# Batch 1's queries loaded in 128-byte blocks and turned by VectorE, and TensorE's opening pauses filled to the end, in a packed-attention and expert-layer kernel

## The chip, the cores and the metric

The kernel runs on one core of a Trainium2 chip, as one launch. The metric is the device time of that launch in microseconds. The core has five engines that run side by side, each through its own list of instructions in order: TensorE (PE, with its weight loads PEld), VectorE (DVE), ScalarE (ACT), GpSimd (POOL) and SyncE (SP), whose list here issues most of the DMA transfers. They wait for each other with semaphores.

## The reference, cut to what matters

Eight batches of eight heads, 576 tokens of 64 values, 32 packed queries `p`. The packed queries attend to the keys and values; then every token's query attends to the packed result, which is both key and value. The output is the input of an expert layer with one expert per token.

```python
def sm_attn(qq, kk, vv):
    s = scale * np.matmul(qq, kk.transpose(0, 1, 3, 2))
    s = s - np.max(s, axis=-1, keepdims=True)
    a = np.exp(s)
    a = a / (np.sum(a, axis=-1, keepdims=True) + 1e-09)
    return np.matmul(a, vv)
p_packed = sm_attn(p, k, v)
x = sm_attn(q, p_packed, p_packed)            # then heads side by side: [8, 576, 512]

logits = np.einsum('bsd,de->bse', x, w_gate)  # 8 experts
# per token s: fresh = argmax of its logits; it keeps the expert of the token before it
# where its local gate is 0.5 or more, else it takes the fresh one; e is that expert
p = softmax(logits[b, s])
h = np.maximum(x[b, s] @ w1[e], 0.0)          # 512 -> 1024
out[b, s] = p[e] * (h @ w2[e])                # 1024 -> 512
```

All is float32. With the inputs used, every token of a batch ends with the expert of that batch's first token, so a batch takes one expert's weights; a branch behind the main part handles others.

## The kernel before

Each batch goes through three parts.

- **Preparation.** Heads are taken in two groups of four, called Q = 0 and 1 in the code ("quads"). Keys and queries are needed with the 64 head values on partitions, so they are turned. `scores` multiplies packed queries and keys (L415), `keys` raises them (ScalarE, L448), turns the weights on TensorE (L458, copies L460), multiplies them with the values (L470), divides (L478, tile `zz`) and turns the result (L485, copy L488, tile `ppT`). `queries` multiplies that with the turned queries (L511, and L520 for the gate), turns the scores on VectorE (L529, tile `sT`), runs a softmax over the 32 packed entries (L540 maximum, L542 subtraction, L544 exponential, L548 to L554 sum and division) and turns them back (L560 or L562, tile `a2t`). `a2t` is split in two numbers of TensorE's fast float format: `a2h` (ScalarE, L568) and the rest `a2l` (L571).
- **The gate.** `gates` (L658, L666) multiplies `a2t` with the gate's weights and picks the expert; `choose` (L601, L604) puts its number in a register of SP. `weights` then loads that expert's first layer `w1t` (L757) and eight pieces of the second, `w2raw` (L766). `pack_weights` multiplies the first layer with `ppT` (L783), casts it (ScalarE, L790, `wph`) and takes the rest (VectorE, L793, `wpl`). For batch 0 an `early_choice` from the first token alone starts the loads sooner.
- **The expert layer,** the main part: `chunks` goes over eight chunks of 128 hidden units. A chunk's first layer is two times six matmuls of 288 tokens (L806), then ScalarE and VectorE split the result in `h` (L816, L821); the second layer is fifteen matmuls or so (L845, L850, L854) with `w2raw` split by L832 (ScalarE) and L834 (VectorE).

The order of every engine's list is set when the kernel is built. `weave` holds threads (generators); each says with `need(...)` what it waits for, a `Clock` with prices for each instruction estimates when that is ready, and `weave` steps the thread that is ready, preferring the main part while it has credit. So a change in one thread moves the rows of others. PSUM has eight banks: three named `bank` for everything short, `acc0` to `acc4` for the second layer's sums, of which `acc1` to `acc3` serve as banks too until the main part begins. A tile of SBUF has a fixed number of buffers per name (`BUFS`: "kv" 4, "qn" 3, "w2raw" 8, "p_in" 2), and a load waits for its buffer.

There are two ways to load and turn keys and queries. `load_tokens` reads a quad with runs of 1,536 bytes into "kv", 576 KB each; `turn_tokens` then turns a head with three TensorE transposes (L365) into a bank, and ScalarE copies it (L369) into "qn". `load_blocks` reads all eight heads with runs of 128 bytes straight into "qn", four transfers of 288 KB; VectorE then turns the 32 by 32 blocks in place (L383 for keys, L496 for queries), one instruction per quad. Batch 0 (`early`) turns its keys on VectorE in tokens form (L351) and its queries by `turn_tokens`; batch 1 (`second`) uses `turn_tokens` for both; batches 2 to 7 use blocks for both. Tokens and blocks leave the tokens in different orders, and L560 and L562 put them right.

`keep_warm` (L214) puts matmuls of zeros into TensorE's list: ten at the start (`WARM`), and, while the main part has not begun, some whenever the planner finds nothing ready: the pause until the next thread is ready, divided by `FILL`.

```python
if x is None:
    x = min(when, key=when.get)
    if at_batch[0] < 0:
        keep_warm(max(0, int((when[x] - now) / FILL)))
    now = max(now, when[x])
```

`now` moves on with every such step, also where the step is not TensorE's. The `Clock` prices such a matmul at about 228 ns.

Of the kernel before, what the change touches and what calls it, by code (L numbers as in the profile page):

```python
# [35 lines left out]

FIRST_BACKLOG = 1400.0

WARM, FILL = 10, 400.0

LAT, SAME = 160.0, 127.0
START, FIRST_LOAD = 5400.0, 1700.0
# [6 lines left out]
FIRST_W2 = {"v": 2, "q": 4}  # L49
# [109 lines left out]
def packed_attn_moe_kernel(  # L159
# [17 lines left out]
    clock = Clock()  # L177
# [138 lines left out]
    def loads(st):  # L316

        b = st["b"]
        if st["early"]:
            st["p"] = load_packs(b, (nc.sync, nc.scalar, nc.scalar))  # L320

            clock.rate = 100.0
            with nc.allow_non_contiguous_dma(reason="512 elements"):
                nc.scalar.dma_start(out=q0[:, :, 0:1], in_=q[0, :, 0:1, :].rearrange("h s d -> d h s"))
            nc.scalar.dma_start(out=wgl[:, :, 0:E], in_=w_gate.rearrange("(h d) e -> d h e", d=D))
            nc.scalar.dma_start(out=wgl[:, :, E:E + 1], in_=w_local.rearrange("(h d) e -> d h e", d=D))
            order = (("k", 0), ("k", 1), ("v", 0), ("v", 1), ("q", 0), ("q", 1))
        else:
            if isinstance(b, int):
                yield need(when=lambda: "loaded" in sts[b - 1] and (b < 2 or "ereg" in sts[b - 2]))  # L330
            order = (("p", 1), ("k", 0), ("k", 1), ("v", 0), ("v", 1), ("q", 0), ("q", 1)) if st["second"] else \
                (("v", 0), ("v", 1), ("p", 1), ("k", 1), ("q", 1))
        for name, Q in order:
            blocks = name in "kq" and not (st["early"] or st["second"])
            if st["second"] and name in FIRST_W2:
                yield need(when=lambda: len(sts[0].get("w2", ())) >= FIRST_W2[name])
            yield need(slot="p_in" if name == "p" else "qn" if blocks else "kv")
            if name == "p":
                st["p"] = load_packs_by_half(b)
                continue  # L340
            x = {"k": k, "v": v, "q": q}[name]
            if blocks:
                st[name] = load_blocks(x, b)
            else:
                st[name, Q] = load_tokens(x, b, Q)
        st["loaded"] = True
# [152 lines left out]
    def queries(st, Q):  # L499
# [54 lines left out]
        nc.vector.tensor_tensor(out=sf, in0=sf, in1=sm.unsqueeze(2).broadcast_to([128, G, NP]), op=ALU.mult)  # L554
        yield need(sT)
        for r in range(2):
            if st["early"] or st["second"]:

                out = a2t.rearrange("a (p i c r) -> a r c p i", p=TP // 32, i=32, c=J3)[:, r]
                nc.vector.transpose(out=out, in_=sT[:, r].rearrange("a (c p) n -> a c p n", c=J3))  # L560
            else:
                nc.vector.transpose(  # L562
                    out=a2t.rearrange("a (m r) -> a r m", r=2)[:, r],
                    in_=sT[:, r].rearrange("a m n -> a (m n)"),
                )
# [182 lines left out]
    def weights(st):  # L748
        yield need(when=lambda: "ereg" in st)
        er = st["ereg"]  # L750
        src = w1[bass.ds(er, 1)].rearrange("o (h x) f -> x (o h) f", h=HQ)
        st["w1"], st["w2"] = [], []
        for fh in range(2):
            yield need(slot="w1t")
            clock.rate = 330.0
            w1t = tile_([128, HQ, 512], F32, "w1t")
            nc.sync.dma_start(out=w1t, in_=src[:, :, 512 * fh:512 * fh + 512])  # L757
            st["w1"].append(w1t)
        for c in range(NC):
            if st.get("early"):  # L760

                yield need(when=lambda: all(c < n or (x, 1) in sts[1] for x, n in FIRST_W2.items()))
            yield need(slot="w2raw")
            raw = tile_([128, DM], F32, "w2raw")
            clock.rate = 330.0
            nc.sync.dma_start(out=raw, in_=w2[bass.ds(er, 1), 128 * c:128 * c + 128, :].rearrange("o r f -> r (o f)"))  # L766
            st["w2"].append(raw)
# [181 lines left out]
    def weave(main):  # L949
# [3 lines left out]
        while main in threads or any(x.batch < 0 for x in threads):  # L953
# [4 lines left out]
            while started < B and started <= max(at_batch[0], 0) + AHEAD:  # L958
                st = sts[started]
                threads.extend(Thread(g, started) for g in (  # L960
                    slots(st), pack_weights(st), *((early_choice(st),) if started == 0 else ()),
                    *((turn_keys(st, 0), turn_keys(st, 1)) if started != 1 else (turn_keys(st, 0), turn_tokens(st, "k"))), scores(st, 0), scores(st, 1), keys(st, 0), keys(st, 1), gate_weights(st) if started == 0 else None, gates(st), *((turn_queries(st, 0), turn_queries(st, 1)) if started > 1 else (turn_tokens(st, "q"),)), queries(st, 0), queries(st, 1),
                ) if g is not None)
                threads.insert(0, Thread(weights(st), started, True))
                started += 1
# [14 lines left out]
            if x is None:  # L980
                x = min(when, key=when.get)
                if at_batch[0] < 0:
                    keep_warm(max(0, int((when[x] - now) / FILL)))
                now = max(now, when[x])
            before = clock.products
            x.step()
# [110 lines left out]
```

## Time and profile before

| | |
|---|---|
| median of 3 runs | 440.71 us (440.34 to 441.14) |
| the profiled execution | 440.03 us |
| its span, first to last instruction | 438.2 us |
| mean granted TensorE clock | 0.984 |
| TensorE busy | 417.8 us, 95% |
| VectorE, ScalarE, GpSimd busy | 303.9, 183.5, 24.9 us |
| moved by DMA | 73.16 MB, mean 167 GB/s |

The profile is of one execution. A line names the source line (L365), the engine, the operation, and output<-input by the names in the code. Times in a timeline are from the span's start; the bracket gives the engine's idle time ahead of the row and what ended it. The "granted clock" is the share of its full clock that TensorE was given. A float32 matmul shows as two records (two passes), a transpose by matmul as one.

### The profile page before, as it was taken

Reading aid. Unit: us, or ns where it says so; the run is one execution under the profiler, and the core shown is the slowest. Engines: PE = TensorE matmul, PEld = TensorE weight load, DVE = VectorE, ACT = ScalarE, POOL = GpSimd, SP = SyncE. Lnnn points to the kernel's source line nnn. Section 1 sums busy time; section 2 is a strip of 40 time slices with the busy share of each in tenths; the row PEclk is TensorE's granted clock in tenths of the full one; section 3 lists DMA queues with packets and bytes.
Section 4 is the critical chain, followed back from the end, with each engine's and each line's share of the span. In section 5 each row is a group of like instructions: output and inputs, shape, how many; then the busy total and the mean of one; then the engine's idle time right before and its main releaser. Section 6 shows DMA issues by size and latency. Waiting matters only on the chain.

```text
span 438.2 us, 10127 instructions
## 1 busy us (share of the span) xinstructions
PE 417.8 (95%) x3928; PEld 326.9 (75%) x3929; DVE 303.9 (69%) x831; ACT 183.5 (42%) x424; POOL 24.9 (6%) x41
## 2 busy tenths in 40 slices
PE   7968999999999999999999999999999999999993
PEld 6756778758866787588876787587876788688882
DVE  4587469876986798648984898648985798444331
ACT  1544534454435553535425553435424453443231
POOL 0000002100110011000110011000110002000000
PEclk9896999999999999999999999999999999999998
DMA  8989699899939995999269991999455210921003
GB/s 191 233 266 259 174 148 137 327 182 226 96 121 321 133 142 179 349 131 194 94 220 240 177 194 49 347 140 141 157 187 186 81 43 10 351 96 37 0 1 114
DMA packets 153942, 73.16 MB, mean 167 GB/s; under 512 B 123680, under 2 KB 132896, under 8 KB 153888
## 3 DMA queue, kind: packets, MB, share of 16 engines
q1 hardware_dynamic: 151760, 72.30, 75.5%
q8 instruction: 33, 0.54, 0.6%
q10 hardware_dynamic: 2128, 0.15, 0.4%
q14 instruction: 21, 0.17, 0.2%
HBM read 63.00 MB, written 9.44 MB: 165 GB/s over the span
## 4 chain that ended last, share of the span: by engine, by line
PE 88%; DVE 5%; DMA 3%; issue 1%; ACT 1%; SPq 0%; POOLq 0%; DVEq 0%; POOL 0%; ACTq 0%
PE acc L845 40%; PE bank L806 24%; PE acc L850 4%; PE bank L783 3%; DMA kv<-in_k_dram 3%; PE acc L854 3%; PE bank L470 3%; PE bank L415 2%; PE bank L458 2%; PE bank L511 2%; PE bank L658 1%; DVE wpl L793 1%; PE bank L365 1%; DVE a2t L560 1%; PE acc L214 0%
## 5 line engine op out<-in xcount | busy, mean ns | idle before, releaser
L845 PE MATMUL acc<-w2s,h 128*128 128x512 f32 x768 | 207.7, 402 | 0.0
L845 PEld LDWEIGHTS acc<-w2s,h 128*128 128x128 f32 x768 | 135.1, 188 | 30.6 <-issue 8.3
L816 ACT ACTIVATE h<-bank 128x288 fp32r<-128x288 f32 x128 | 52.7, 412 | 117.9 <-PE bank L806 108.1
L821 DVE SCALAR_TENSOR_TENSOR h<-bank,h 128x288 fp32r<-128x288 f32 (+2 forms) x192 | 61.3, 347 | 50.1 <-ACT h L816 49.3
L806 PEld LDWEIGHTS bank<-a2h,wph 128*128 128x128 f32 x256 | 47.0, 191 | 23.9 <-issue 3.6
L806 PE MATMUL bank<-a2h,wph 128*128 128x288 f32 x256 | 57.9, 308 | 5.5 <-DVE wpl L793 1.8
L806 PE MATMUL bank<-a2l,wph 128*128 128x288 f32 x256 | 55.5, 299 | 0.0
L806 PE MATMUL bank<-a2h,wpl 128*128 128x288 f32 x256 | 55.3, 298 | 0.0
L834 DVE TENSOR_TENSOR w2s<-w2raw,w2s 128x512 fp32r<-128x512 f32 x64 | 47.7, 745 | 8.3 <-ACT w2s L832 8.2
L806 PEld LDWEIGHTS bank<-a2l,wph 128*128 128x128 f32 x256 | 41.7, 191 | 0.0
L806 PEld LDWEIGHTS bank<-a2h,wpl 128*128 128x128 f32 x256 | 41.7, 191 | 0.0
L832 ACT CAST w2s<-w2raw 128x512 fp32r<-128x512 f32 x64 | 39.4, 616 | 0.2
L571 POOL TENSOR_TENSOR a2l<-a2t,a2h 128x576 fp32r<-128x576 f32 x14 | 20.5, 1462 | 328.7 <-ACT a2h L568 328.7
L793 DVE TENSOR_TENSOR wpl<-bank,wph 128x512 fp32r<-128x512 f32 x31 | 20.1, 685 | 13.3 <-ACT wph L790 13.3
L790 ACT CAST wph<-bank 128x512 fp32r<-128x512 f32 x31 | 16.7, 590 | 28.0 <-PE bank L783 26.9
L850 PE MATMUL acc<-w2s,h 128*128 128x512 f32 x64 | 26.9, 420 | 0.0
L854 PE MATMUL acc<-w2s,h 128*64 128x512 f32 x64 | 25.3, 395 | 0.0
L783 PE MATMUL bank<-w1t,ppT 64*32 64x512 f32 x248 | 17.4, 601 | 2.7 <-DVE sm L550 1.6
L529 DVE STREAM_TRANSPOSE sT<-bank 128x288 f32<-128x288 f32 x30 | 12.8, 462 | 10.1 <-ACT gate L527 9.4
L448 ACT ACTIVATE a<-a,nb 128x576 f32<-128x576 f32 x16 | 12.5, 779 | 14.9 <-DVE nb L433 14.9
L460 ACT COPY a1T<-bank 96x384 f32<-96x384 f32 x28 | 13.3, 477 | 10.5 <-PE bank L458 10.0
L383 DVE STREAM_TRANSPOSE qn<-qn 128x1152 f32<-128x1152 f32 x12 | 16.4, 1364 | 0.1
(146 smaller groups left out, 434.7 us busy)
## 6 DMA issues: line engine op xcount, KB each, us to landing
w1t<-in_moe_w_dram SPq DMA_DIRECT2D x16, 1024.0 KB, 6.3
w2raw<-in_moe_w_dram SPq DMA_DIRECT2D x64, 256.0 KB, 7.7
kv<-in_v_dram SPq DMA_DIRECT2D x16, 576.0 KB, 10.7
out_dram<-o SPq DMA_DIRECT2D x32, 256.0 KB, 3.8
qn<-in_k_dram SPq DMA_DIRECT2D x24, 288.0 KB, 7.5
qn<-in_q_dram SPq DMA_DIRECT2D x24, 288.0 KB, 6.9
kv<-in_k_dram SPq DMA_DIRECT2D x4, 576.0 KB, 6.9
kv<-in_q_dram SPq DMA_DIRECT2D x4, 576.0 KB, 11.2
```

The costliest lines, as they stand in the source:

```text
L571: eng.tensor_tensor(out=a2l, in0=a2t, in1=a2h.bitcast(F32), op=ALU.subtract)
L783: nc.tensor.matmul(out=ts[Q][32 * h:32 * h + 32, :], lhsT=st["ppT"][Q][rows, 32 * h:32 * h + 32], rhs=w1t[rows, h], start=True, stop=True,)
L790: nc.scalar.copy(out=hi[:, Q], in_=ts[Q])
L793: nc.vector.tensor_tensor(out=lo[:, Q], in0=ts[Q], in1=hi[:, Q].bitcast(F32), op=ALU.subtract)
L806: nc.tensor.matmul(out=t[:, :HALF], lhsT=st["wp"][c // 4][wi][:, Q, fs], rhs=a2[ai][Q][:, ts], start=(n == 0), stop=(n == 5),)
L816: nc.scalar.activation(out=h[:, HALF * half:HALF * half + HALF], in_=t[:, :HALF], func=AF.Relu)
L821: nc.vector.scalar_tensor_tensor(out=h[:, dst:dst + z - a], in0=t[:, a:z], scalar=0.0, in1=h[:, HALF * half + a:HALF * half + z].bitcast(F32),
L832: nc.scalar.copy(out=w[:, 0], in_=raw)
L834: nc.vector.tensor_tensor(out=w[:, 1], in0=raw, in1=w[:, 0].bitcast(F32), op=ALU.subtract)
L845: nc.tensor.matmul(out=acc, lhsT=hs[hi], rhs=w[:, wi], start=(c == 0 and n == 0), stop=(c == NC - 1 and n == 2),)
L850: nc.tensor.matmul(out=acc, lhsT=h[:, 512:S + TAIL], rhs=w[:, 0], start=(c == 0), stop=False, skip_group_check=True,)
L854: nc.tensor.matmul(out=acc[0:TAIL], lhsT=h[:, 512:S], rhs=w[:, 1], start=False, stop=(c == NC - 1), skip_group_check=True,)
```

## The change

Five edits, shown whole. Batch 1's queries are one load in blocks (`load_blocks`, tile "qn") instead of two in tokens; they are turned by `turn_queries` (two L496 on VectorE) instead of `turn_tokens`; its `a2t` is written by L562 instead of L560, in block order; the wait of batch 0's weight loads is for that new load. And a pause is counted from TensorE's own planned end instead of `now`, in pieces of 240 ns instead of 400.

```diff
-WARM, FILL = 10, 400.0
+WARM, FILL = 10, 240.0
...
-            order = (("p", 1), ("k", 0), ("k", 1), ("v", 0), ("v", 1), ("q", 0), ("q", 1)) if st["second"] else \
+            order = (("p", 1), ("k", 0), ("k", 1), ("v", 0), ("v", 1), ("q", 1)) if st["second"] else \
                 (("v", 0), ("v", 1), ("p", 1), ("k", 1), ("q", 1))
         for name, Q in order:
-            blocks = name in "kq" and not (st["early"] or st["second"])
+            blocks = name in "kq" and not st["early"] and not (st["second"] and name == "k")
...
         for r in range(2):
-            if st["early"] or st["second"]:
+            if st["early"]:
...
             if st.get("early"):
 
-                yield need(when=lambda: all(c < n or (x, 1) in sts[1] for x, n in FIRST_W2.items()))
+                yield need(when=lambda: all(c < n or x in sts[1] for x, n in ((("v", 1), FIRST_W2["v"]), ("q", FIRST_W2["q"]))))
...
-                    ... *((turn_queries(st, 0), turn_queries(st, 1)) if started > 1 else (turn_tokens(st, "q"),)), ...
+                    ... *((turn_queries(st, 0), turn_queries(st, 1)) if started else (turn_tokens(st, "q"),)), ...
...
                 if at_batch[0] < 0:
-                    keep_warm(max(0, int((when[x] - now) / FILL)))
+                    keep_warm(max(0, int((when[x] - clock.engine("PE")) / FILL)))
```

What it moves is seen in the lists of instructions. The names are tiles with a running number; in the first two pairs the bank's own number stands ahead of the underscore, and the bracket names the engines or DMA queues that a row waits for.

TensorE, from the last filling to the main part's first rows. Before:

```order
L214 MATMUL acc4_66<-warm_64 128x128 x5
L783 MATMUL bank1_565<-w1t_453,ppT_313 32x512 [waits DMAHW3_49,Activation_49]
L783 MATMUL bank1_565<-w1t_453,ppT_313 32x512 x3
L783 MATMUL bank2_566<-w1t_453,ppT_324 32x512 [waits Activation_49]
L783 MATMUL bank2_566<-w1t_453,ppT_324 32x512 x3
L806 MATMUL bank0_583<-a2h_123,wph_533 128x288 [waits DVE_49,Activation_49]
```

And now:

```order
L214 MATMUL acc4_66<-warm_64 128x128 x10
L783 MATMUL bank2_620<-w1t_472,ppT_331 32x512 [waits DMAHW3_49,Activation_49]
L783 MATMUL bank2_620<-w1t_472,ppT_331 32x512 x3
L783 MATMUL bank0_621<-w1t_472,ppT_342 32x512 [waits DVE_49]
L783 MATMUL bank0_621<-w1t_472,ppT_342 32x512 x3
L806 MATMUL bank1_632<-a2h_123,wph_565 128x288 [waits DVE_49,Activation_49]
```

Ten fillings stand there instead of five, and the last L783 writes bank0, which VectorE's first L793 (of `bank0_567`) has to read first.

VectorE at the same place. Before:

```order
L793 TENSOR_TENSOR wpl_534<-bank0_535,wph_533 128x512 [waits PE_49]
L793 TENSOR_TENSOR wpl_534<-acc1_536,wph_533 128x512 [waits PE_49]
L793 TENSOR_TENSOR wpl_564<-bank1_565,wph_563 128x512 [waits Activation_49]
L793 TENSOR_TENSOR wpl_564<-bank2_566,wph_563 128x512 [waits Activation_49]
L834 TENSOR_TENSOR w2s_590<-w2raw_455,w2s_590 128x512 [waits DMAHW4_49,Activation_49]
```

And now:

```order
L793 TENSOR_TENSOR wpl_566<-bank0_567,wph_565 128x512 [waits PE_49]
L793 TENSOR_TENSOR wpl_566<-bank1_568,wph_565 128x512 [waits PE_49]
L834 TENSOR_TENSOR w2s_639<-w2raw_474,w2s_639 128x512 [waits DMAHW4_49,Activation_49]
L793 TENSOR_TENSOR wpl_615<-bank2_620,wph_614 128x512 [waits PE_49]
L793 TENSOR_TENSOR wpl_615<-bank0_621,wph_614 128x512 [waits PE_49]
```

L834 has moved ahead of the last two L793. Its ScalarE partner L832 still stands behind all four L790.

TensorE in batch 0's expert layer, where batch 1 is prepared. Before:

```order
L845 MATMUL acc_643<-w2s,h 128x512 x3
L470 MATMUL bank_795<-kv,a1T 32x64 x24
L365 MATMUL bank_824<-ident,kv 128x96 x3
L845 MATMUL acc_662<-w2s,h 128x512 x3
L485 MATMUL bank_848<-ident,zz 128x128
L365 MATMUL bank_853<-ident,kv 128x96 x3
L845 MATMUL acc_680<-w2s,h 128x512 x3
L365 MATMUL bank_862<-ident,kv 128x96 x3
L511 MATMUL bank_866<-qn,ppT 32x288 x4
```

And now:

```order
L845 MATMUL acc_693<-w2s,h 128x512 x3
L458 MATMUL bank_826<-ident,a_618 96x128 x3
L845 MATMUL acc_712<-w2s,h 128x512 x3
L845 MATMUL acc_730<-w2s,h 128x512 x3
L470 MATMUL bank_842<-kv,a1T 32x64 x24
L806 MATMUL bank_870<-a2h,wph 128x288 x2
L806 MATMUL bank_870<-a2l,wph 128x288 x2
L806 MATMUL bank_870<-a2h,wpl 128x288 x2
L485 MATMUL bank_877<-ident,zz 128x128
```

The eight groups of L365 that turned batch 1's queries are gone, and the rows around them stand closer.

More of the change, by code (lines that the diff above doesn't have):

```diff
@@ L961, in weave @@
                     slots(st), pack_weights(st), *((early_choice(st),) if started == 0 else ()),
-                    *((turn_keys(st, 0), turn_keys(st, 1)) if started != 1 else (turn_keys(st, 0), turn_tokens(st, "k"))), scores(st, 0), scores(st, 1), keys(st, 0), keys(st, 1), gate_weights(st) if started == 0 else None, gates(st), *((turn_queries(st, 0), turn_queries(st, 1)) if started > 1 else (turn_tokens(st, "q"),)), queries(st, 0), queries(st, 1),
+                    *((turn_keys(st, 0), turn_keys(st, 1)) if started != 1 else (turn_keys(st, 0), turn_tokens(st, "k"))), scores(st, 0), scores(st, 1), keys(st, 0), keys(st, 1), gate_weights(st) if started == 0 else None, gates(st), *((turn_queries(st, 0), turn_queries(st, 1)) if started else (turn_tokens(st, "q"),)), queries(st, 0), queries(st, 1),
                 ) if g is not None)
```

## The prediction

> **What bounds the kernel now.** I read the page first: busy times and the slices of the granted clock.
>
> ```profile
> span 438.2 us, 10127 instructions
> ...
> PE 417.8 (95%) x3928; PEld 326.9 (75%) x3929; DVE 303.9 (69%) x831; ACT 183.5 (42%) x424; POOL 24.9 (6%) x41
> ...
> PEclk9896999999999999999999999999999999999998
> ```
>
> TensorE works 95% of the span, so a matmul taken out of the main part is worth its own time, and a busy VectorE or DMA costs only where TensorE waits. TensorE is idle for 20.4 us (438.2 - 417.8), and apart from the last slice the clock row has its dips in slices 2 and 4 (11 to 22 and 33 to 44 us). So the second view is the busy time in stretches. I set their edges where the clock changes, 3.4 us apart.
>
> ```profile
> 8.06:11.47 3.41, 2.42 (x98) 1.00 1.09 212
> 11.47:14.88 3.41, 3.41 (x30) 0.50 1.10 235
> ...
> 28.50:31.94 3.44, 1.90 (x23) 1.00 1.05 396
> 31.94:35.35 3.41, 1.60 (x21) 1.00 1.07 305
> 35.35:38.77 3.42, 2.62 (x11) 0.50 1.07 257
> 38.77:42.18 3.41, 3.41 (x42) 0.50 1.08 264
> ```
>
> The columns are the stretch, its length, TensorE's busy time and instructions, granted clock, DMA share and GB/s. The clock is whole or half. It fell behind a stretch with 1.60 us of matmul and did not fall behind one with 1.90. It also fell behind 2.42 us at 8.06, where 96 of the 98 records are small 32x32 score matmuls. The half-clock stretches end behind one that was full (3.41 of 3.41). So three stretches run at half clock, and the two from 35.35 are the start of the main part.
>
> The third view is TensorE in order of time through the opening (start, length, idle before it).
>
> ```profile
> 1.09 6.18 PE L214 MATMUL acc<-warm 128*128 128x128 f32 x38 [1.09 <-DVE warm L207]
> ...
> 8.80 1.15 PE L415 MATMUL acc<-kv,p_in 32*32 32x192 f32 x48 [1.53 <-DVE p_in L351]
> ...
> 10.62 1.32 PE L415 MATMUL bank<-kv,p_in 32*32 32x192 f32 x48 [0.25 <-DVE kv L351]
> 11.87 1.65 PE L214 MATMUL acc<-warm 128*128 128x128 f32 x6
> 13.31 1.49 PE L458 MATMUL acc<-ident,a 128*96 128x128 f32 x6
> ...
> 15.70 1.55 PE L470 MATMUL bank<-kv,a1T 96*32 96x64 f32 x96
> ...
> 23.57 0.44 PE L365 MATMUL acc<-ident,kv 96*128 96x96 f32 x3 [1.28 <-DMA kv<-in_k_dram]
> ...
> 31.06 1.38 PE L214 MATMUL acc<-warm 128*128 128x128 f32 x10
> ```
>
> A warm-up matmul is two records. Ten records take 1.38 us at full clock: five at about 0.23, and the last one's tail. At half clock it is near twice that (six records in 1.65).
>
> **The change, part by part.** *More filling before the scores.* The list of instructions has 30 warm-ups instead of 19 ahead of the first scores, then 3 for 1, 7 for 3 and one more. The 11 extra end the first run at about 9.8 instead of 7.27, and the pipelined scores start near 9.5, not 8.80. With 3 warm-ups between, the second scores go from 10.62 to about 11.2, and the 7 at full clock (1.6 us) bring L458 to 14.0 against 13.31. Against that, 8.06:11.47 is now full, so I expect no half clock at 11.47. L458 up to the start of L470 took 2.39 us, nearly all at half clock; at full clock with two warm-ups it is about 1.7, so L470 starts at 15.7 as before. The cover for an error of some tenths is the transfer of batch 1's keys: TensorE waited 1.28 us for it at 23.57, the DMA share is above 1 in those stretches, and the transfers ahead of it keep the queues full. I take 0, bounds -0.3 and +0.7.
>
> *From 24.75 to the first hidden-layer product.* VectorE sets the end here.
>
> ```profile
> 24.75 0.48 DVE L529 STREAM_TRANSPOSE sT<-acc 128x288 f32<-128x288 f32 x1 [0.96 <-PE bank L511]
> ...
> 25.52 1.37 DVE L540 TENSOR_REDUCE mx<-sT 128x18 f32<-128x576 f32 x2
> ...
> 35.32 0.68 DVE L793 TENSOR_TENSOR wpl<-bank,wph 128x512 fp32r<-128x512 f32 x1
> ...
> 37.71 0.68 DVE L834 TENSOR_TENSOR w2s<-w2raw,w2s 128x512 fp32r<-128x512 f32 x1
> ```
>
> And ScalarE, in the same form:
>
> ```profile
> 34.66 1.07 ACT L790 CAST wph<-bank 128x512 fp32r<-128x512 f32 x2
> 35.62 0.63 ACT L832 CAST w2s<-w2raw 128x512 fp32r<-128x512 f32 x1
> ```
>
> In the new order the first L540 stands ahead of L529 and fills the idle 0.96; the chain up to the first L793 gets about 0.6 shorter (half of 1.37, less a wait for ScalarE), so that L793 ends at 35.4 instead of 36.0. But the new order makes two waits. The last L783 now goes into bank0, which the first L793 has to free; before, it had a bank of its own and ran at 33.54. And L834 stands ahead of the last two L793, and waits for L832, which stands behind the last L790 on ScalarE.
>
> ```profile
> 33.54 1.09 PE L783 MATMUL bank<-w1t,ppT 64*32 64x512 f32 x16 [1.10 <-DMA w1t<-in_moe_w_dram]
> ...
> 39.30 1.08 PE L658 MATMUL bank<-a2t,gate 128*32 128x128 f32 x16
> ...
> 40.52 0.85 PE L806 MATMUL bank<-a2h,wph 128*128 128x288 f32 x2
> ...
> 42.13 0.89 PE L845 MATMUL acc<-w2s,h 128*128 128x512 f32 x3
> ```
>
> So: last L783 35.45 to 36.5 (1.09 was for two halves side by side, and one alone is hardly shorter), L790 to 37.1, L832 to 37.7, L834 to 38.4, L793 to 39.0. The first six L806 run meanwhile; the second six need the bank that this L793 frees, at 39.05. Six L806 cost 1.61 at half clock (40.52 to 42.13), so 0.8 at full; the gate matmuls 1.22 (39.30 to 40.52), so 0.6. With the clock whole, L845 starts at 39.05 + 0.8 + 0.6 + 0.8 = 41.25, 0.9 earlier than 42.13.
>
> Is it whole? The 10 warm-ups for 5 between the pairs of L783, and half of the last pair gone, leave 31.94:35.35 with about 1.6 + 0.85 = 2.45 us: no fall at 35.35. The next stretch then holds one L783 half (1.05) and six L806 (0.8): 1.85, between the 1.60 that fell and the 1.90 that didn't, and its L783 use half of the rows. I hold a fall at 38.77 for likelier than not. Then the second L806 (1.6) and the gate (1.2) run at half clock to 41.85, the third ends at 42.8, 0.7 later than before. The Trainium skill ("TensorE: Matmul & The Clock Gate", Part 1) states that the clock halves after at least one idle window of about 3.4 us. By that rule no stretch here would fall and the first sum, -0.9, holds; but the trace disagrees, with falls behind stretches that held 1.60 and 2.42 us of matmul.
>
> *Batch 1's queries.* Eight groups of three transposes leave TensorE, and eight copies leave ScalarE, which has room.
>
> ```profile
> 48.08 0.41 PE L365 MATMUL bank<-ident,kv 96*128 96x96 f32 x3
> 48.27 0.47 PE L850 MATMUL acc<-w2s,h 128*128 128x512 f32 x1
> ...
> 51.13 0.53 PE L806 MATMUL bank<-a2h,wph 128*128 128x288 f32 x2 [0.51 <-ACT a1T L460]
> ...
> 53.43 0.88 PE L470 MATMUL bank<-kv,a1T 96*32 96x64 f32 x48
> ...
> 56.36 0.41 PE L365 MATMUL bank<-ident,kv 96*128 96x96 f32 x3
> 56.71 0.72 PE L511 MATMUL bank<-qn,ppT 64*32 64x288 f32 x16
> ...
> 58.17 0.53 PE L806 MATMUL bank<-a2h,wph 128*128 128x288 f32 x2 [0.73 <-ACT qn L369]
> ```
>
> A group costs from 0.19 (48.08 to 48.27) to 0.35 us (56.36 to 56.71); the eight add up to 1.9, between 1.5 and 2.8. The 0.73 waited for such a copy and goes; the 0.51 waited for a copy that now has the ScalarE queue to itself, and six L806 stand elsewhere. Together -1.24, bound 0 if other bank waits take their place. VectorE gets two turns:
>
> ```profile
> L496 DVE STREAM_TRANSPOSE qn<-qn 128x1152 f32<-128x1152 f32 x12 | 16.4, 1369 | 0.0
> ```
>
> That is 2 x 1.37 = 2.7 us, less what the plainer a2t transposes save, on an engine that is idle for 31% of the span: 0, bound +2.7.
>
> The load of 1.18 MB (8 x 576 x 64 values) changes from two pieces in "kv" to four in "qn" with runs of 128 bytes (columns: stretch, length, clock, DMA share, GB/s):
>
> ```profile
> 34.00:44.00 10.00, 0.66 1.08 248
> ...
> 48.00:56.00 8.00, 1.00 0.40 95
> 58.00:72.00 14.00, 1.00 1.42 140
> ```
>
> 1.18 MB at 140 GB/s (58 to 72, nearly all block loads) are 8.4 us; from 34 to 44, with token and weight loads, the rate is 248, or 4.8. So the queries, and the four second-layer loads behind them on SP, land some 3.6 us later than before: with the old load the engines were quiet from 48, so at up to 51.6. The cover is the quiet stretch from 48 to 56 and that chunk 4's weights are used behind 56. What SP has next, batch 2's values, waited for a "kv" slot and now has one. I take 0.
>
> *The seam to batch 1.* Both pairs of L783 now stand nearly side by side just ahead of batch 1's first L806, and half of the second waits for the first's L793: about 1.1 us of stall and of work no longer side by side. Before, it had idle times of 0.47 and 0.25:
>
> ```profile
> 91.96 0.53 PE L806 MATMUL bank<-a2h,wph 128*128 128x288 f32 x2 [0.47 <-DVE zz L478]
> ...
> 95.48 0.54 PE L806 MATMUL bank<-a2h,wph 128*128 128x288 f32 x2 [0.25 <-DVE wpl L793]
> ```
>
> So +0.4, bounds 0 and +1.
>
> **The sum.** -1.9 - 1.24 + 0.4 = -2.74, and the opening: +0.7 with one half-clock stretch, together -2.06; -0.9 without, -3.6. The profiled execution took 440.03 (span 438.2 and 1.83 around it), 0.68 below the median of the runs, 440.71. On that median: 438.65, and 437.1.
>
> **The rivals.** *No half clock at all* (1.85 us is enough, or the windows lie otherwise): 437.1. For it, the 1.90 that held. By the Trainium skill's rule above it would be this case.
> *Half clock from 35.35 as before*: L783 alone takes 2.1, the chain reaches 40.0, half-clock products follow, L845 starts at 43.5, 1.4 later: -1.35, 439.4. Against it, the filling.
> *What leaves TensorE comes back as waits*: the two turns of 1.37 us stand in VectorE's row ahead of the products' second halves (L821) that free the banks. If TensorE paid them whole, -2.06 + 2.74 = +0.7, 441.4: no change. Against it, TensorE has almost 2 us of other rows there.
> *The queries land late* (the other side): VectorE takes its rows in turn, and the first L496 stands ahead of the second zz (L478), which reads the L470 of 53.43 and which TensorE needs next. That L470 ends at 54.2, by my sum some 0.7 earlier; less the 1.37 of the turn, the queries must have landed by 52.1. Beyond that every microsecond is TensorE's: landing at 55.1 or later eats the 2.06 and 0.9 more, over 441.6. The estimate of 51.6 is for everything queued behind them too, so the queries should be well ahead of it.
>
> **Chances.** Forecast 0.42, no half clock 0.25, half clock from 35.35 0.15, waits 0.12, late queries 0.06. Under 0.2% (0.88 us) a measurement of this kernel can't tell from none. Faster by more holds the first three, less a little for bounds: 0.78; same 0.15; slower 0.07. The time is 438.6. Range 436.8 (no half clock and the transposes' upper price) to 440.5 (waits for most of the turns).
>
> **What would show it.** Right: clock whole at 11.47 and 35.35; TensorE idle near 2 us ahead of the second six L806, with L793 as releaser; no L365 behind 31 us; L845's first start at 41 to 43. Wrong: a half-clock stretch elsewhere in the opening, DMA as L496's releaser, or new idle time between 45 and 60.

## The result, and the profile after

The changed kernel takes 437.41 us (436.90 to 438.29) against 440.52 us before: 0.9941 of the time, 95% interval 0.9920 to 0.9962. On another chip, in the run `e8_after_again` below, it was 436.74 against 440.57, 0.9912 (0.9887 to 0.9936). It is faster, by 3.1 to 3.8 us; 2.06 were forecast. The profiled execution of the first comparison is its longest, 438.29 us with a span of 436.5; so `e8` (span 434.8) is used beside it.

The page of the changed kernel: TensorE's idle time fell from 20.4 to 12.3 us, while its busy time is 6.4 us longer: 72 more warm-up records, 24 transposes fewer. VectorE's turns (L496) are 14 instead of 12.

```profile
span 436.5 us, 10221 instructions
...
PE 424.2 (97%) x3976; PEld 331.9 (76%) x3977; DVE 305.3 (70%) x833; ACT 181.3 (42%) x416; POOL 24.2 (6%) x41
...
PEclk9997899999999999999999999999999999999997
...
L496 DVE STREAM_TRANSPOSE qn<-qn 128x1152 f32<-128x1152 f32 x14 | 19.2, 1368 | 0.0
```

The stretches of the opening (stretch, length, TensorE busy and instructions, granted clock, DMA share, GB/s). The half-clock times of before, one stretch from 11.47 and two from 35.35, are gone. The clock falls at about 39.2 instead, and in this execution it stays half up to 46.0.

```profile
11.47:14.88 3.41, 3.41 (x69) 1.00 1.11 228
31.94:35.35 3.41, 3.41 (x44) 1.00 1.07 326
35.35:38.77 3.42, 2.62 (x22) 1.00 1.08 244
38.77:42.18 3.41, 2.27 (x18) 0.56 1.31 209
42.18:45.60 3.42, 3.42 (x37) 0.50 1.07 109
45.60:49.00 3.40, 3.40 (x40) 0.94 1.32 137
```

TensorE in order of time, the rows that answer to those of before:

```profile
1.09 8.85 PE L214 MATMUL acc<-warm 128*128 128x128 f32 x60 [1.09 <-DVE warm L207]
...
9.87 1.15 PE L415 MATMUL acc<-kv,p_in 32*32 32x192 f32 x48
...
31.07 0.41 PE L365 MATMUL acc<-ident,kv 96*128 96x96 f32 x3
31.41 1.09 PE L783 MATMUL bank<-w1t,ppT 64*32 64x512 f32 x16
...
36.30 1.06 PE L783 MATMUL bank<-w1t,ppT 64*32 64x512 f32 x8 [0.38 <-DVE wpl L793]
...
39.91 0.85 PE L806 MATMUL bank<-a2h,wph 128*128 128x288 f32 x2 [1.56 <-DVE wpl L793]
...
42.87 0.85 PE L806 MATMUL bank<-a2h,wph 128*128 128x288 f32 x2
...
44.48 1.48 PE L845 MATMUL acc<-w2s,h 128*128 128x512 f32 x3
```

The second half of the last L783 waits for the bank, and the second six L806 wait 1.56 us for the last two L793, which on VectorE stand behind L834, which waits for ScalarE:

```profile
38.56 0.69 DVE L834 TENSOR_TENSOR w2s<-w2raw,w2s 128x512 fp32r<-128x512 f32 x1 [1.72 <-ACT w2s L832]
39.17 1.28 DVE L793 TENSOR_TENSOR wpl<-bank,wph 128x512 fp32r<-128x512 f32 x2
```

To see where the time went I compare the starts of the same rows in the traces (us). "Queries only", "filling only" and the others are the experiments below.

| start of | before | after | e8, after again | e1, queries only | e2, filling only | e4, stall filled | e3, own banks | e9, zz first |
|---|---|---|---|---|---|---|---|---|
| first L845 | 42.13 | 44.48 | 43.66 | 40.98 | 42.42 | 42.52 | 40.04 | 40.58 |
| batch 0, chunk 4 | 66.47 | 65.82 | 64.34 | 63.03 | 65.77 | 63.20 | 64.25 | 62.36 |
| batch 1, chunk 0 | 91.96 | 90.99 | 89.52 | 88.31 | 90.91 | 88.38 | 89.37 | 88.78 |
| batch 1, chunk 4 | 116.54 | 115.73 | 114.25 | 113.04 | 115.64 | 113.12 | 114.11 | 113.52 |
| batch 2, chunk 0 | 144.72 | 143.19 | 141.71 | 140.53 | 143.11 | 140.60 | 141.61 | 141.02 |
| span | 438.2 | 436.5 | 434.8 | 433.8 | 436.5 | 433.6 | 434.6 | 434.0 |

The opening loses 1.5 to 2.4 us up to the first L845; the stretch from there to chunk 4, where the transposes were, wins 3.66 in `e8` (24.34 to 20.68). The result is a loss and a larger gain. Not all of the gain is the queries': `e2`, which keeps the transposes, takes 23.35 us for the same stretch, 0.99 less than before.

### The profile page after: what moved, and what is told of

Read it like the earlier page. It is cut to its first block, busy times and chain, and to the rows that moved or that the text cites. A ratio compares the mean times of both kernels' runs of the same rounds, so it can differ in the third digit from the quotient of the medians.

```text
span 436.5 us, 10221 instructions
## 1 busy us (share of the span) xinstructions
PE 424.2 (97%) x3976; PEld 331.9 (76%) x3977; DVE 305.3 (70%) x833; ACT 181.3 (42%) x416; POOL 24.2 (6%) x41
## 4 chain that ended last, share of the span: by engine, by line
PE 92%; DVE 3%; DMA 2%; ACT 1%; issue 1%; POOLq 0%; POOL 0%; DVEq 0%
PE acc L845 41%; PE bank L806 24%; PE bank L783 4%; PE acc L214 4%; PE acc L850 4%; PE acc L854 3%; PE bank L470 3%; PE bank L415 2%; PE bank L458 2%; PE bank L511 2%; DMA kv<-in_k_dram 2%; PE bank L658 1%; ACT wph L790 1%; DVE wpl L793 1%; DVE qn L383 0%
## 5 line engine op out<-in xcount | busy, mean ns | idle before, releaser
L845 PE MATMUL acc<-w2s,h 128*128 128x512 f32 x768 | 208.4, 402 | 0.0
L845 PEld LDWEIGHTS acc<-w2s,h 128*128 128x128 f32 x768 | 135.2, 189 | 30.6 <-issue 7.9
L806 PEld LDWEIGHTS bank<-a2h,wph 128*128 128x128 f32 x256 | 46.7, 190 | 22.0 <-DVE wpl L793 3.4
L806 PE MATMUL bank<-a2h,wph 128*128 128x288 f32 x256 | 57.7, 307 | 3.0 <-DVE wpl L793 1.6
L806 PE MATMUL bank<-a2l,wph 128*128 128x288 f32 x256 | 55.3, 297 | 0.0
L806 PE MATMUL bank<-a2h,wpl 128*128 128x288 f32 x256 | 55.1, 297 | 0.0
L834 DVE TENSOR_TENSOR w2s<-w2raw,w2s 128x512 fp32r<-128x512 f32 x64 | 47.7, 745 | 7.8 <-ACT w2s L832 7.8
L806 PEld LDWEIGHTS bank<-a2l,wph 128*128 128x128 f32 x256 | 41.5, 190 | 0.0
L806 PEld LDWEIGHTS bank<-a2h,wpl 128*128 128x128 f32 x256 | 41.4, 190 | 0.0
L832 ACT CAST w2s<-w2raw 128x512 fp32r<-128x512 f32 x64 | 39.4, 615 | 0.2
L793 DVE TENSOR_TENSOR wpl<-bank,wph 128x512 fp32r<-128x512 f32 x32 | 20.5, 684 | 12.3 <-ACT wph L790 12.3
L790 ACT CAST wph<-bank 128x512 fp32r<-128x512 f32 x32 | 17.3, 590 | 26.8 <-PE bank L783 26.8
L214 PE MATMUL acc<-warm 128*128 128x128 f32 x146 | 21.2, 298 | 1.1 <-DVE warm L207 1.1
L214 PEld LDWEIGHTS acc<-warm 128*128 128x128 f32 x146 | 19.3, 209 | 2.3 <-issue 1.4
L783 PE MATMUL bank<-w1t,ppT 64*32 64x512 f32 x256 | 19.3, 601 | 0.4 <-DVE wpl L793 0.4
L496 DVE STREAM_TRANSPOSE qn<-qn 128x1152 f32<-128x1152 f32 x14 | 19.2, 1368 | 0.0
```

What stands on the lines that cost most here:

```text
L214: nc.tensor.matmul(out=warm_ps[:, :128], lhsT=warm, rhs=warm, start=True, stop=True)
L783: nc.tensor.matmul(out=ts[Q][32 * h:32 * h + 32, :], lhsT=st["ppT"][Q][rows, 32 * h:32 * h + 32], rhs=w1t[rows, h], start=True, stop=True,)
L790: nc.scalar.copy(out=hi[:, Q], in_=ts[Q])
L793: nc.vector.tensor_tensor(out=lo[:, Q], in0=ts[Q], in1=hi[:, Q].bitcast(F32), op=ALU.subtract)
L806: nc.tensor.matmul(out=t[:, :HALF], lhsT=st["wp"][c // 4][wi][:, Q, fs], rhs=a2[ai][Q][:, ts], start=(n == 0), stop=(n == 5),)
L832: nc.scalar.copy(out=w[:, 0], in_=raw)
```

## The experiments

Every version ran beside the kernel before on the same chip; a ratio is to that.

**The two parts apart.** `e1` is the changed kernel with the old filling:

```diff
-WARM, FILL = 10, 240.0
+WARM, FILL = 10, 400.0
-                    keep_warm(max(0, int((when[x] - clock.engine("PE")) / FILL)))
+                    keep_warm(max(0, int((when[x] - now) / FILL)))
```

> Only the queries' part of the change; pauses are filled as before, so the opening's list is that of before. Theory A (the queries carry the gain, the filling costs): eight groups of transposes (1.9 us) and the two waits of 1.24 us go, 3.1 us, and the clock dips of before stay: about 0.7% under the kernel before, 437.4 us beside 440.5; the trace of the changed kernel shows 3.6 us between the second chunk and the fifth, which would be 436.9. Theory B (the filling carries the gain through the clock, the transposes' time comes back as waits): within 0.2% of before.

Measured: 436.61 us, 0.9923 (0.9893 to 0.9953). `e2` is the kernel before with the same two lines changed the other way round.

> Only the filling part of the change; batch 1's queries are loaded in tokens and turned by TensorE as before. Theory A: the opening of the changed kernel with its bank wait and the half clock that follows it: the first L845 at about 44.5 us instead of 42.1, so 1 to 3 us slower than before, 441.5 to 443.5. Theory B: 1 to 3 us faster than before.

Measured: 439.28 us, 0.9966 (0.9943 to 0.9990). The queries alone bring all that both parts bring together. The filling alone brings 1.1 us by the medians and 1.5 by the ratio, where I had expected a loss. The gains do not add up; I take it that this is because either part also changes the order of the opening. `e1` has no wait of L806 for the last L793, only one of 1.51 us for an earlier L793 ahead of its first L806, as the kernel before has it (1.52). It starts its first L845 3.5 us ahead of the changed kernel's. In `e2` the wait for the last L793 stands:

```profile
39.82 0.54 PE L806 MATMUL bank<-a2h,wph 128*128 128x288 f32 x2 [1.55 <-DVE wpl L793]
...
42.42 0.86 PE L845 MATMUL acc<-w2s,h 128*128 128x512 f32 x3
```

Yet in this trace the clock stays whole (columns as above), after the same wait behind which it fell in the changed kernel. In other executions of `e2` it may have fallen: five of the twelve have a mean clock of 0.990 or 0.991, against 0.997 in the traced one.

```profile
35.35:38.77 3.42, 2.53 (x22) 1.00 1.09 244
38.77:42.18 3.41, 2.36 (x43) 1.00 1.07 287
```

These two have the edges of the kernel before. In one trace all changes of the clock lie whole multiples of 3.41 us apart (before: 11.46, 14.88, 35.35, 42.18 and, at the end, 434.7), so the stretches at whose ends it changes can be set from any one of them; they lie elsewhere in each of the executions compared here. In the changed kernel the stretch that ends with the fall is 35.79 to 39.20 and holds 2.18 us of matmul; in `e8`, below, it is 35.98 to 39.39, with 2.06. In `e2`, set from the last fall at 433.45, the stretch from 37.50 to 40.92 holds only 1.87, and the clock stays whole.

**Does that fall belong to the kernel or to the execution?** `e8` is the changed kernel once more, unedited.

> The changed kernel once more, for comparison with the other versions on one chip and for the number of half-clock stretches from execution to execution. Theory A (the stall of 1.56 us at 38.4 to 39.9 decides whether the clock falls, and differs between executions): granted clocks of single executions lie in groups about 0.004 apart (one stretch of 3.4 us at half clock is 1.7 of 436 us), from 0.997 (none) over 0.993 (one) to 0.987 (two and more), and the time falls by about 1 us from group to group; median 437 to 438 us. Theory B (the clock does not differ): one clock, times spread without relation to it.

Measured: 436.74 us, 0.9912. Over the two comparisons the changed kernel ran ten times: 435.8 and 435.9 us at a mean granted clock of 0.996 to 0.997; 436.6 to 437.5 (seven) at 0.993 to 0.994; 438.3 at 0.987. One stretch of 3.41 us at half clock takes 3.41 / 2 / 436 = 0.004 off the mean, so I read these as no, one, and two half-clock stretches. Two of the ten were traced: the last has two, and `e8` (0.993) has one. The mean also holds the end of the execution, where the clock falls behind the last matmuls, 0.002 to 0.006 in the traces here; so 0.994 alone decides nothing: `e11`'s trace has one stretch at 0.994, `e9`'s none. The one of `e8`:

```profile
38.77:42.18 3.41, 2.42 (x22) 0.59 1.32 209
42.18:45.60 3.42, 3.42 (x51) 0.91 0.90 98
```

So the same wait cost a half-clock stretch in most executions and, by this reading, none in two, and one is worth about 1 us. The Trainium skill ("TensorE: Matmul & The Clock Gate", Part 1) says that the window of about 3.4 us runs freely and that the count of slow matmuls changes from run to run; these ten agree. That a whole idle window is needed before the clock halves, the traces contradict: here it fell behind windows with 2.18 and 2.06 us of matmul. Nor does the matmul time of the window alone decide it, since 1.87 held in `e2`.

**Filling the stall.** `e4` puts six warm-up matmuls between the first and the second six L806 of batch 0:

```diff
+                    if isinstance(b, int) and b == 0 and c == 0 and half == 1:
+                        keep_warm(6)
```

> The changed kernel with six more warm-up matmuls (1.4 us) between the first and the second six L806, in the stall for L793 of 1.56 us; the stall itself stays. If the half clock comes from the idle time in the stretch from 35.8 to 39.2, it is gone: the second six L806 still start at 39.9, the first L845 at 42.1 instead of 44.5, and the time is 2 to 3 us under the changed kernel, 434.5 to 435.5. If the clock falls whatever stands in the pause, the time is the changed kernel's or up to 0.5 us more.

Measured: 436.43 us, 0.9917 (0.9888 to 0.9947). The clock is whole in the trace, and L806 starts no sooner:

```profile
38.21 1.50 PE L214 MATMUL acc<-warm 128*128 128x128 f32 x12
39.92 0.54 PE L806 MATMUL bank<-a2h,wph 128*128 128x288 f32 x2 [0.21 <-DVE wpl L793]
...
42.52 0.86 PE L845 MATMUL acc<-w2s,h 128*128 128x512 f32 x3
```

Six of the seven executions had 0.995 to 0.998, one 0.994. The clock came out as expected, the time did not: against `e8`'s 436.74 the difference of 0.3 us is inside the spread, and it is not below the changed kernel's two executions with a whole clock (435.9). The seven lie from 435.4 to 437.0 us without a half-clock stretch to explain it. So of the filling of the stall the clock is shown, and a gain in time is not.

The traces of `e4` and `e2` make a pair: the same filling of pauses, first L845 at nearly the same time, clock whole in both. From the first L845 to batch 1's first L806 `e2` takes 48.49 us and `e4` 45.86, and the spans differ by 2.9. That is the price of the queries in these traces: 2.6 us, of which 0.5 are two waits in `e2` (0.29 for L460, 0.22 for L745) and, by difference, 2.1 the eight groups of transposes, 0.27 each (0.30 if only the stretch up to chunk 4 is taken). The trace of `e4` is of its fastest execution; by the medians of the executions at 0.995 or more the two differ by 2.0, by all by 2.9.

**Taking the wait away.** In `e3` the early L783 of batch 0 take `acc` banks first, so that the last one needs not wait for an L793:

```diff
-            ts = [bank() for Q in range(NQ)]
+            tags = [x[2] for x in sorted(free_banks(), key=lambda y: (st["early"] and y[2] in banks, y))[:NQ]]
+            ts = [psum(x) for x in tags]
```

> The changed kernel; only the first pair of batch 0's L783 takes the spare banks acc3 and acc2, so that the second pair has bank0 and bank1 to itself. In the list, L834 then stands behind all four L793. Theory A (the bank wait and what it does to the clock cost the opening): no idle 1.56 us ahead of the second six L806, the clock whole from 5 to the end of the main part, the first L845 near 39.8 us instead of 44.5: 4 to 5 us under the changed kernel, 432.5 to 433.5. Rival (VectorE's chain sets the start whatever the banks, and the half clock comes anyway): the first L845 at 42 or later, gain below 2 us.

Measured: 435.47 us, 0.9896 (0.9861 to 0.9931); once more on another chip (`e11`):

> The version with own banks once more, unchanged, as the one to which the version with the moved row is compared on the same chip: 434.5 to 436 us, with the idle time of 1.2 to 1.8 us ahead of the second L485.

436.50 us, 0.9896 (0.9858 to 0.9934). That is not the gain of 4 to 5 us that theory A named: by the medians `e3` is 1.9 us under the first measurement of the changed kernel and `e11` 0.2 under `e8`, and the intervals overlap. The place itself went as expected. The first L845 starts at 40.04 us, 3.6 ahead of `e8`, but at chunk 4 only 0.1 is left of it. VectorE and TensorE in the trace of `e3` show where it went:

```profile
53.16 1.38 DVE L496 STREAM_TRANSPOSE qn<-qn 128x1152 f32<-128x1152 f32 x1 [2.97 <-DMA qn<-in_q_dram]
54.47 0.31 DVE L478 TENSOR_SCALAR zz<-bank,rs 128x128 f32<-128x128 f32 x1
```

```profile
54.83 0.35 PE L485 MATMUL bank<-ident,zz 128*128 128x128 f32 x1 [1.78 <-DVE zz L478]
...
57.25 1.21 PE L511 MATMUL bank<-qn,ppT 64*32 64x288 f32 x16
```

The queries land at 53.2. The first turn waits for them, zz stands behind it in VectorE's list, TensorE waits for zz, and half clock follows (55.0 to 58.4). This is the prediction's "queries land late". In `e1` it is there too, with 1.14 us ahead of L485. In `e11`, the same kernel as `e3`, it is smaller than the expected 1.2 to 1.8: the first turn starts at 51.75, and the clock stays whole up to 88.4.

```profile
53.41 0.33 PE L485 MATMUL bank<-ident,zz 128*128 128x128 f32 x1 [0.54 <-DVE zz L478]
```

So the landing, and with it the price, differs between executions. In the changed kernel the slow opening hides it: there L478's input comes at 57.2, 4 us behind the landing in `e3`.

**The price of that order.** `e9` is `e3` with one row moved on VectorE: the first turn behind the second zz, everything else where it was. The planner accounts for the turn at its old place and the instruction is written a row later.

```diff
+        if st["second"] and Q == 0:
+            clock.later(qT)
+            st["later"] = qT
...
+        if "later" in st:
+            qT = st.pop("later")
+            nc.vector.transpose(out=qT, in_=qT)
```

> The version with own banks (435.47 us) with one row moved: on VectorE the first query turn of batch 1 (L496) comes behind the second zz (L478) instead of ahead of it; every other row of every engine stands where it stood. Theory A (the order of these two rows is what the late queries cost): L485 starts near 52.9 without the 1.78 us of idle time, the first L511 near 55.1 instead of 57.25, no half-clock stretch behind 54, and since the seam to batch 1 keeps its order, nothing is given back: 1.5 to 2.5 us below the same version without the move, 433 to 434 us. Theory B (the turned queries are needed just as early): the idle time moves to L511, difference under 0.5 us.

Measured: 434.22 us, 0.9860 (0.9817 to 0.9902), 2.3 us under `e11` on the same chip, though the intervals overlap. Among the executions with a mean clock of 0.995 or more, the four of `e9` took 434.0 to 434.3 us and the three of `e11` 435.2 to 435.9. VectorE and then TensorE (line numbers are 9 to 19 higher: L487 is zz, L499 the transpose of zz, L529 the scores, L825 the product, L802 L783's):

```profile
52.66 0.35 DVE L487 TENSOR_SCALAR zz<-bank,rs 128x128 f32<-128x128 f32 x1 [1.94 <-PE bank L479]
53.39 1.38 DVE L494 STREAM_TRANSPOSE qn<-qn 128x1152 f32<-128x1152 f32 x1 [0.38 <-DMA qn<-in_q_dram]
```

```profile
53.43 0.27 PE L499 MATMUL bank<-ident,zz 128*128 128x128 f32 x1
...
54.87 0.81 PE L529 MATMUL bank<-qn,ppT 64*32 64x288 f32 x16
...
56.58 0.50 PE L825 MATMUL bank<-a2h,wph 128*128 128x288 f32 x2 [0.90 <-ACT w2s L851]
...
87.76 1.09 PE L802 MATMUL bank<-w1t,ppT 64*32 64x512 f32 x16 [1.89 <-DMA w1t<-in_moe_w_dram]
```

The wait ahead of the zz transpose and the half clock are gone, as theory A had it; 0.90 comes back ahead of the next product. Its row names ScalarE's w2s (55.93 to 56.55) as releaser; but a product needs a free bank, not w2s, and on VectorE the L840 that frees one stands behind the second turn (55.95 to 56.43). I take it for that, though the trace doesn't tell the two apart. The last row names what is late next, now that TensorE comes sooner: the first layer's weights of batch 1. `e11` shows the same wait (1.81), `e3` doesn't. Where the 2.3 us come from, the traces of `e9` and `e11` don't show: at chunk 4 `e9` is 1.8 us ahead (62.36 to 64.20), but at batch 1's first L806 it has none of it left (88.78 to 88.69), and the spans (434.0 to 435.3) part only there, where `e11` has a half-clock stretch from 88.4. The traced execution of `e9`, 435.74 us, is one of its slower ones. That the row is the cause rests on the times, since the edits of the two differ in it alone. `e9` is the best version that I ran.

An attempt at the same with the planner's own means, `e5`, held the turns until both zz were turned:

```diff
-        yield need(when=lambda: "q" in st and "a2t" in st)
+        yield need(when=lambda: "q" in st and "a2t" in st and (not st["second"] or None not in st["ppT"]))
```

> The version with own banks for the first pair of L784 (435.47 us), with the first query turn (L496) of batch 1 now placed behind both zz (L478) on VectorE; later rows of that batch shift by a few places too. Theory A (the order costs, not the landing): the queries land near 53.2 us as in that version, but zz no longer stands behind the turn that waits for them, so the second transpose of zz (L485) starts near 52.9 instead of 54.83 and its 1.78 us of idle time and the half-clock stretch behind it (55 to 58.8) are gone; 433.0 to 434.3 us. Theory B (TensorE needs the turned queries just as early): the idle time comes back ahead of the first L511 or of a later L807, 435 to 436 us.

Measured: 439.46 us, 0.9995 (0.9969 to 1.0022). The place itself went as theory A said: L485 at 52.72 without a wait, and chunk 4 at 60.64, 3.6 ahead of `e3`. But the planner moved other rows too, and TensorE waits at the seam to batch 1. I take it that batch 0's products, moved forward, were missing there as cover; no run tests it:

```profile
84.96 0.90 PE L458 MATMUL bank<-ident,a 128*96 128x128 f32 x6 [0.90 <-ACT a L448]
...
89.37 0.57 PE L458 MATMUL bank<-ident,a 128*96 128x128 f32 x3 [1.08 <-ACT ppT L488]
```

Batch 1's first L806 starts at 91.09 there against 89.37 in `e3`: 3.6 us won, then 5.3 lost.

**What the filling is worth without the wait.** `e6` is `e5`, and `e10` is `e9`, each with the old filling (the two lines of `e1`).

> The same as the kernel with the turns behind both zz, but with the filling of the opening as before (FILL 400 and now in the call of keep_warm); the rest of the order is the same. Theory A (the filling is worth something by itself, as the kernel with only the filling showed: 1.1 us): one or two half-clock stretches return between 8 and 30 us, the time is 0.5 to 1.5 us above that of the kernel with the turns behind zz. Theory B (the opening waits for batch 1's keys and for VectorE in any case): the two are within 0.4 us of each other.

Measured: 442.49 us, 1.0040 (1.0016 to 1.0064), 3.0 above `e5` on the same chip.

> The version with own banks and the moved row, with the filling before (FILL 400, now); the order differs from it only up to the first L784. Theory A (the filling keeps the clock whole in the opening and that is worth time): half-clock stretches return between 8 and 30 us and the time is 1 to 3 us above the version with the new filling. Theory B (the opening is set by the keys' landing and by VectorE): within 0.4 us of it.

Measured: 434.93 us, 0.9884 (0.9830 to 0.9937), 0.7 above `e9`; its mean clocks are 0.975 to 0.988 against 0.987 to 0.998. So, by the mean clocks (0.965 to 0.988 in `e6`, 0.981 to 0.992 in `e5`), the old filling costs half-clock stretches in both; 3.0 is above the 0.5 to 1.5 that theory A of `e6` named, and 0.7 lies between the two theories of `e10`. What the filling is worth (3.0, 0.7, 1.1 in `e2`, nothing between `e1` and the changed kernel) is not settled by these runs, and 0.7 is not told from none.

**What a turn on VectorE costs.** `e7` makes each of the two query turns of batch 1 three times.

```diff
-        nc.vector.transpose(out=qT, in_=qT)
+        for again in range(3 if st["second"] else 1):
+            nc.vector.transpose(out=qT, in_=qT)
```

> The changed kernel with each of batch 1's two query turns made three times (an odd number of turns gives the same values): 4 more transposes of 1.37 us on VectorE, 5.5 us, whose second zz stands behind the first three. Theory A (VectorE has room there: 1.7 to 2.1 us idle of every 4 between 44 and 56): most of it is covered, and only the wait of the second zz shows, since a turn that ends near 59.3 instead of 56.6 is 2 us later than its input; 437.5 to 439.5 us. Theory B (a turn is paid by TensorE): 441 to 443 us.

Measured: 443.52 us, 1.0074 (1.0049 to 1.0098). That falls on theory B's side, but by another way: at chunk 4 it is at 63.00 us, where `e4` is at 63.20, and the loss comes at the seam (batch 1's first L806 at 99.22). The planner saw the longer turns and moved rows, so this run doesn't price a turn. `e12` hides the extra turns from the planner, so that only VectorE's list differs:

```diff
         nc.vector.transpose(out=qT, in_=qT)
+        if st["second"]:
+            nc.pop_inst_callback()      # the planner's clock sees nothing of these two
+            nc.vector.transpose(out=qT, in_=qT)
+            nc.vector.transpose(out=qT, in_=qT)
+            nc.push_inst_callback(clock.note)
```

> The changed kernel with each query turn of batch 1 made three times (the same values), and the order of all other rows kept: 5.5 us more on VectorE between 55 and 64 us. The first three turns end near 59.3, so the zz that stands behind them comes 2 us late (L485 at 59.6 instead of 58.0), and the second three end near 63.7, 5 us later than before, with the L822 of two halves behind them. Theory A (VectorE's idle time covers a turn): up to 1 us more than the changed kernel. Theory B (a turn more is paid nearly whole once zz and L822 stand behind it): 3 to 5.5 us more.

Measured: 442.65 us, 1.0042 (1.0012 to 1.0071), 5.9 us above `e8` for 5.5 us more on VectorE. VectorE's and TensorE's rows:

```profile
59.64 0.31 DVE L478 TENSOR_SCALAR zz<-bank,rs 128x128 f32<-128x128 f32 x1
```

```profile
60.01 0.48 PE L485 MATMUL bank<-ident,zz 128*128 128x128 f32 x1 [1.54 <-DVE zz L478]
...
64.62 0.51 PE L811 MATMUL bank<-a2h,wph 128*128 128x288 f32 x2 [0.94 <-ACT w2s L837]
```

zz comes 2.4 us later than in the changed kernel, as expected; TensorE waits 1.54 for it, falls to half clock (60.0 to 63.4), and waits again, 0.94, while the rows of VectorE that free a bank (64.0 to 64.5) stand behind the second set of turns. The two waits and half of the 3.4 us add up to 4.2. Between the first product of the second layer and chunk 4 the trace takes 4.3 us more than the changed kernel's (44.78 to 70.38, against 44.48 to 65.82; both have two half-clock stretches in the opening). The other 1.6 of the 5.9 are not located. Theory B holds for turns beyond the two. VectorE's idle time, 5.0 of the 16 us from 50 to 66 in the changed kernel, did not help, since rows that TensorE waits for stand behind the turns.

## Why the prediction was right, and which terms were off

It forecast 438.6, in 436.8 to 440.5, by a loss in the opening and a larger gain in the transposes; that is what the traces show, and 437.41 lies in the range. The size is partly luck. The second measurement, 436.74, falls just under the range, and both are nearer to the rival without half clock (437.1) than to the forecast, though most executions, `e8` among them, have the one half-clock stretch of the forecast. The sum as written, -2.74 + 0.7, is -2.04, not -2.06. Its terms, against before, by the table: forecast -2.06, measured -3.4 of the span of `e8`.

- **The clock at 11.47 and 35.35**: whole, as forecast, and no L365 behind 31.07. The fall was put at 38.77 and came at 39.2 and 39.4, behind the wait that was named, with the releaser that was named (1.56 idle, "near 2"). The reason given for it did not hold: the edges were those of another execution, and the test was whether a stretch holds more than 1.60 to 1.90 us of matmul. The clock fell behind 2.18 and 2.06 and stayed whole behind 1.87 (`e2`).
- **The opening up to the first L845, +0.7**: measured +1.53 in `e8`, +2.35 in the profiled execution with two stretches. The mis-sized step is the chain ahead of it: L793 was to end 0.6 sooner than before and the second six L806 to start at 39.05; they start at 39.76 (39.91); the first L793 starts no sooner than before (35.41 and 35.56, against 35.32). L783 started at 31.41 instead of 30.04, since fillings and transposes held TensorE until then, and batch 1's keys came 0.5 us later. The cover on which the 0 for more filling rested, the 1.28 us of waiting for those keys, was thinner than I took it for: 0.38 to 0.48 us of it are left. L845 "at 41 to 43" was missed: 43.66 and 44.48.
- **Transposes and their two waits, -3.14**: measured -3.66 between the first L845 and chunk 4, where no wait is left. But `e2`, with the transposes, has 0.99 of it, and of the two waits of 1.24 only 0.29 stands in its trace: most of that part came with the filling's order. The queries' own part is the 2.67 between `e2` and `e4`, with 0.27 to 0.30 a group instead of 0.24. So the term was named rightly and put down to the wrong half of the change in part.
- **The turns on VectorE, 0**: no wait stands at them in the changed kernel. `e12` shows how little was left of that cover.
- **The load, 0**: right by the time, wrong by its working. The queries were to land by 51.6 at the latest. In the five traces where their user waits for them they landed between 52.8 and 53.5 (`e1`, `e3`, `e5`, `e9`) and at 51.75 (`e11`). SP needed 16.6 us to issue the four pieces, and the rate between 42.18 and 45.60, where nothing else was being loaded, was 109 GB/s instead of the 140 taken:

```profile
30.61 16.60 SPq L288 DMA_DIRECT2D qn<-in_q_dram  x4
...
47.39 5.01 SPq L766 DMA_DIRECT2D w2raw<-in_moe_w_dram  x4
```

  In four of the five the threshold of 52.1 was passed; in the changed kernel the landing itself isn't seen, since nothing waits for it. That rival, given 6 in 100, did not strike because the opening was late too: two errors that hid each other, by luck. Its price where the opening is faster is a wait of 1.78 us in `e3`, 1.14 in `e1` and 0.54 in `e11`, and in `e3` half clock behind it.
- **The seam, +0.4**: from chunk 4 of batch 0 to chunk 4 of batch 1, -0.16. The two idle times of before (0.47, 0.25) went, and none is shown ahead of the second pair of L783, though its row lasts 1.90 us where the first lasts 1.09.
- **Behind the seam, not forecast: -1.1** (-0.72 up to batch 2, -0.39 to the end). Of it, 0.49 is one wait (before, then `e8`):

```profile
128.96 0.51 PE L806 MATMUL bank<-a2h,wph 128*128 128x288 f32 x2 [0.81 <-DVE df L716]
```

```profile
125.98 0.50 PE L806 MATMUL bank<-a2h,wph 128*128 128x288 f32 x2 [0.32 <-DVE df L716]
```

- **The rival without half clock (437.1)** was, by the mean clock, the case in two executions of ten, at 435.9. It and the forecast differ by 1.2 us in these, by 1.55 in my sum.

## What to carry to other kernels

Before a transfer is made slower, ask which row stands behind its first user in that engine's list: in `e3` VectorE, which takes its rows in turn, handed a late load to work that has nothing to do with it, and moving one row (`e9`) took 1.5 to 2.3 us off the time. A gain in one place shifts what is late next (a wait, then a load, then the next batch's weights), and where a planner sets the order it may move the loss to a later stage (`e5`, `e7`); compare the starts of the same rows through the whole trace, not the one place. An engine that is idle for a third of the time may still have no room for more (`e12`), if rows for which the bound engine waits stand behind the new ones.

## What I had not expected of the hardware

The same kernel with the same wait loses its clock in one execution and not in another: 0, 1 or 2 stretches of 3.4 us, 435.8 to 438.3 us. The medians hold a mix, so for a change of less than about 1 us in the opening of this kernel the mean clock of each execution has to be read beside its time; and even that leaves a spread of 1.6 us in `e4`. In `e2` the clock stayed whole behind a stretch with 1.87 us of matmul in 3.4; in the changed kernel it fell behind one with 2.18.
